# Router scratch in a PSUM bank, and 64-column products set between 512-column ones, in a fused attention and expert kernel

## The chip, the cores and the metric

The kernel runs on one core of a Trainium2 chip, in one launch. The metric is the device time of an execution in microseconds (us); less is better. Three runs of the kernel before took 832.63, 827.26 and 828.55 us, median 828.55.

The engines are named as in the profile: PE (TensorE, matrix products; PEld are its weight loads), DVE (VectorE), ACT (ScalarE), POOL (GpSimd) and SP (SyncE, which issues DMAs).

## The reference

Causal attention over 8 batches, 8 heads, 576 positions and 64 features, with a bias from a running sum of `s`; then a mixture of 8 experts, where each of the 4608 tokens goes to the one expert of the largest logit.

```python
def _attn_ref(q, k, v, s):
    scores = scale * np.matmul(q, k.transpose(0, 1, 3, 2))
    cum = np.cumsum(np.maximum(s, 0.0), axis=-1)
    bias = -(cum[:, :, :, None] - cum[:, :, None, :])
    scores = np.where(causal, -1000000000.0, scores + np.minimum(bias, 0.0))
    attn = np.exp(scores - np.max(scores, axis=-1, keepdims=True))
    attn = attn / (np.sum(attn, axis=-1, keepdims=True) + 1e-09)
    return np.matmul(attn, v)
def _moe_ref(x, expert_emb, tau, w1, w2):
    logits = xn @ en.T / tau                       # rows of x and of expert_emb normalised
    expert_idx = np.argmax(logits, axis=1)
    gate_w = softmax(logits)[np.arange(N), expert_idx]
    for e in range(E):
        mask = expert_idx == e
        h = np.maximum(x[mask] @ w1[e], 0.0)       # 512 -> 1024
        out[mask] = gate_w[mask, None] * (h @ w2[e])   # 1024 -> 512
```

## The kernel before

**Attention half.** The 64 heads are steps `n`, eight to a batch. A step computes scores for the row maxima of a later head (tiles `s`, read by DVE at lines 369, 406 and 409), the scores and exponentials of head `n` (tiles `ta`, `tb` in the pool `ps_t`), and the products with V of head `n - 2` (`pv`, lines 525 to 527), which add up in one fixed PSUM bank, `om`, columns 0 to 364. POOL subtracts the rounded exponentials from the full ones (line 251) for a second, low part of the products. Two or three steps behind, DVE normalises `om` into the token rows `xt` (lines 538 to 550).

When a batch of eight heads is done, `router(b, xt)` puts small steps into a queue of tasks, from which each step takes up to four at its end: `sume` adds up the logits (line 79 in the trace) into `L`, 128x40; `sel1` to `sel4` pick the best expert; `sel5` (line 622) compares and writes the one-hot rows `oh`; a few products on PE count ranks into `om` (columns 368 to 415), and DVE adds them up (lines 638 to 650); then POOL scatters the token rows to their experts' places in memory. `L`, `T` and `w` are parts of an SBUF tile named `idx`, which POOL fills and from which eight DMAs read a block of zeros early on, in `setup4`.

**Expert half.** An expert has places for 640 tokens, in tiles of 128. Its first layer is eight blocks `m` of 128 hidden features (`l1`, line 891): 12 products of 512 columns (tokens 0 to 511), since each number is kept as a high and a low half and three of the four products count. Tokens 512 to 575 are 12 products of 64 columns for each of the eight blocks, 96 in one burst (`l1a` calls `lpart`, line 915), issued behind block 5 for expert 1 and behind block 2 from expert 2 on. Tokens from 576 on are taken only where an expert has so many (`l1b`, a branch on PE). `lrect` applies the ReLU to the 64-column sums. The second layer (`l2`, line 967) has 24 products of 512 columns for each 128 tokens; its last tile is `l2t`, whose result is finished in the next expert's first layer (`l2u`). Expert 0 starts while the last batch is still being routed: its tokens are taken in three parts, `l1` with `lo` at 0, 256 and 384.

The order of the work on every engine is the order in which the program is written. Beside the first layer of expert `e`, DVE and ACT convert the second layer's weights to halves (lines 867 and 875); `xload` has POOL gather the token rows of expert `e + 1` (line 737; the first three behind block 2), and `xprep` splits and transposes them by DMAs that SP issues (line 788).

[...] The first layer's `h` uses half of a `ps_t` tile.

Of the kernel before, what the change touches and what calls it, by code (L numbers as in the profile page):

```python
# [8 lines left out]
F32 = mybir.dt.float32  # L9
# [8 lines left out]
PSUM = bass.MemoryType.PSUM  # L18
# [96 lines left out]
def main(ctx, tc, qkh, qkc, vtin, s_in, emb, tau, w1h, w2h, out, shared, nb):  # L115
# [5 lines left out]
    ps_s = ctx.enter_context(tc.tile_pool(name="ps_s", bufs=2, space=PSUM))  # L121
    ps_t = ctx.enter_context(tc.tile_pool(name="ps_t", bufs=2, space=PSUM))
    ps_m, om = shared["ps_m"], shared["om"]
# [474 lines left out]
    def router(b, xt):  # L598
        R = {}

        def sume():
            R["L"] = IX["L"].rearrange("p (j e) -> p j e", j=5)
            esum(nc, R["L"], xt[:, :, 0:XW])
# [5 lines left out]
        def sel2():  # L609
            T = R["T"] = IX["T"].rearrange("p (j e) -> p j e", j=5)  # L610
            nc.vector.tensor_tensor(T, R["L"], R["m"][:, 0].unsqueeze(2).to_broadcast([128, 5, NE]), op=ALU.is_ge)

# [3 lines left out]
        def sel4():  # L616
            R["w"] = IX["w"]
            nc.vector.tensor_reduce(R["w"], R["T"], AX.X, ALU.max)

# [174 lines left out]
    def pxm():  # L794
        return ps_m.tile([128, 512], F32, tag="m", name="pxm")

    def pxs():
        return ps_s.tile([128, 512], F32, tag="s", name="pxs")
# [84 lines left out]
    def l1(m, e, lo, hi, mid=None):  # L883
        wH, wL = ready(1, e, m)
        xH, xL = X[("H", e)], X[("L", e)]
        if isinstance(xL, tuple):
            xL = xL[lo > 0 or e > 0]
        h = (pxs() if e == 0 and m in {0: (1, 3, 5, 7), SPL: (1, 3, 5), SPM: (1, 2, 5)}[lo] else ps_t.tile([128, 2, 512], F32, tag="t", name="h")[:, 0])[:, 0:hi - lo]
        for c in range(4):
            for k, (w, x) in enumerate(((wH, xH), (wH, xL), (wL, xH))):  # L890
                nc.tensor.matmul(h, w[:, 128 * c:128 * c + 128], x[:, c, lo:hi], start=(c == 0 and k == 0), stop=(c == 3 and k == 2))  # L891
            if c == 1 and mid:
                mid()
        hH, hL = (t[:, lo:hi] for t in htile(m))
        nc.scalar.activation(hH, h, AF.Relu)
        nc.vector.scalar_tensor_tensor(hL, h, 0.0, hH, op0=ALU.max, op1=ALU.subtract)
# [10 lines left out]

    def lpart(e, u, h):
        xH, xL = X[("H", e)], X[("L", e)][1]
        lo = MAIN + HALF * u  # L910
        for m in range(8):
            wH, wL = ready(1, e, m)
# [10 lines left out]

    def l1a(e):
        h = pxs()
        lpart(e, 0, h)
        lrect(0, h)

    def l1b(e, h):
# [6 lines left out]
    def l1t():  # L936
        h = ps_t.tile([128, 2, 512], F32, tag="t", name="h")
        with tc.If(X["n", 0] == 1) as arm:
            for u in range(2):
                lpart(0, u, h[:, u])  # L940
        with arm.Else():
            for u in range(2):
                nc.tensor.matmul(h[:, u], wt(1, 0)[0][:, 0:128], X[("H", 0)][:, 0, 0:MAIN], start=True, stop=True)
        X["h", 0] = h
# [33 lines left out]
    def l2(e, t, mid={}):  # L978
        y = pxs()
        l2m(t, y, mid)  # L980
        l2o(e, t, y)
# [489 lines left out]
    for u in range(2):  # L1471
        lrect(u, X["h", 0][:, u])
    for e in range(NE):
        nx = e + 1 < NE
        w2, w1 = 16 * e + 8, 16 * e + 16
        for m in range(8):
# [3 lines left out]
            if e == 1 and m == 0:  # L1480
                l2o(0, NTL - 1, X["y", 0])
            if e and m == (5 if e == 1 else 2):
                l1a(e)
                size(e)
# [44 lines left out]
            if e == 3 and m == 4:  # L1529
                shared["total"] = nc.values_load(shared["ci"][0:1, NE - 1:NE], min_val=0, max_val=NT // 128)  # L1530
        if e:
            l1b(e, pxs())
        for t in range(0 if e else NF, NTL):
# [165 lines left out]
```

## Time and profile before

| | |
|---|---|
| runs | 832.63, 827.26, 828.55 us, median 828.55 |
| the profiled execution | 827.8 us, of which the span from first to last instruction is 826.1 us |
| PE busy | 769.1 us, 93% of the span |
| DVE, ACT, POOL busy | 556.5, 569.2 and 395.3 us |
[...]
| memory traffic | 140 GB/s over the span |

Times in the trace count from the start of the span. The attention half lasts to about 380 us, the expert half to the end. A row of the timeline gives the start, the length, the engine, the line of the kernel, the operation, what it writes and reads, how many equal ones stand behind each other, and in brackets the idle time of the engine ahead of it with what ended that. A product's length in the timeline is its latency; products overlap, so the distance of two starts is what one costs. Where the idle time is put down to "issue", the engine waited for nothing that the profile shows.

### The profile page before, as it was taken

The page shows a single profiled execution, that of the slowest core. Times are in us where ns is not written, and L with a number is a line of the kernel's source. Part 1 is how long each engine was busy: PE and PEld are TensorE (multiplying, and loading weights), DVE is VectorE, ACT ScalarE, POOL GpSimd, SP SyncE. Part 2 cuts the span into 40 slices and gives each one's busy share as a digit, 9 for nine tenths or more (in the row PEclk, how much of TensorE's full clock was granted, in tenths as well). Part 3 has the DMA queues.
Part 4 walks back from the last instruction along what each step waited for, and adds up shares of the span by engine and source line. Part 5 has one row for each costly group of instructions (what it writes and reads, how often), then busy time and mean ns, then how long its engine had stood idle before and what let it go on. Part 6 is the DMA issues. An engine that isn't in the chain of part 4 may idle for free. (4 is left out here: it accounts for less than half of the span.)

```text
span 826.1 us, 20954 instructions
## 1 busy us (share of the span) xinstructions
PE 769.1 (93%) x7998; PEld 552.9 (67%) x7998; DVE 556.5 (67%) x1818; ACT 569.2 (69%) x1029; POOL 395.3 (48%) x375
## 2 busy tenths in 40 slices
PE   8998898989989898999789998989989989999997
PEld 4798897989989897988454554545444544554554
DVE  7787788787878888898557765654555556645621
ACT  9898688897969897887467865827637649376410
POOL 9997596887869796873432121220221112202001
PEclk9999899999989999999989999999999989999999
DMA  7798779595949797764534855643744746534001
GB/s 162 158 196 169 137 177 193 133 209 132 199 113 216 150 209 150 177 207 129 185 99 154 190 160 158 163 153 108 177 145 112 188 151 140 177 113 124 25 13 53
DMA packets 76002, 124.01 MB, mean 150 GB/s; under 512 B 38823, under 2 KB 39231, under 8 KB 75032
## 3 DMA queue, kind: packets, MB, share of 16 engines
q0 software_dynamic: 19632, 69.69, 36.2%
q1 hardware_dynamic: 56260, 52.84, 24.1%
q8 instruction: 71, 1.16, 0.6%
q14 instruction: 39, 0.32, 0.1%
HBM read 93.99 MB, written 21.49 MB: 140 GB/s over the span
## 5 line engine op out<-in xcount | busy, mean ns | idle before, releaser
L251 POOL TENSOR_TENSOR PL<-P 128x576 f16<-128x576 f32 (+2 forms) x128 | 205.1, 1709 | 31.9 <-ACT P L500 21.7
L891 PE MATMUL h<-xH,wt 128*128 128x512 f16 (+2 forms) x560 | 155.7, 360 | 0.8 <-DVE hq L922 0.3
L891 PEld LDWEIGHTS <-wt 128*128 128x128 f16 x960 | 86.8, 100 | 84.6 <-issue 11.9
L975 POOL DMA_INDIRECT out<-Kx,xj x39 | 44.1, 1130 | 195.2 <-DVE Kx L974 165.4
L361 PE MATMUL s<-qkb 96*128 96x288 f32 (+4 forms) x272 | 98.7, 377 | 22.4 <-DVE M L369 21.8
L525 PE MATMUL om<-vh,P 128*128 128x73 f16 x960 | 110.5, 201 | 3.0 <-DVE xt L550 2.3
L737 POOL DMA_INDIRECT Qx<-xs,idx x40 | 44.3, 1107 | 140.1 <-ACT vjunk L830 70.7
L526 PE MATMUL om<-vl,P 128*128 128x72 f16 x960 | 109.7, 199 | 0.0
L527 PE MATMUL om<-vh,PL 128*128 128x73 f16 x960 | 109.5, 200 | 0.0
L526 PEld LDWEIGHTS <-P 128*128 128x128 bf16 x960 | 96.5, 101 | 4.2 <-issue 3.6
L525 PEld LDWEIGHTS <-P 128*128 128x128 bf16 x960 | 95.7, 101 | 0.5 <-DVE xt L550 0.3
L527 PEld LDWEIGHTS <-PL 128*128 128x128 f16 x960 | 95.7, 100 | 0.0
L891 PE MATMUL h<-xL,wt 128*128 128x512 f16 (+1 forms) x264 | 94.9, 366 | 0.0
L967 PE MATMUL pxs<-wt,hq 128*128 128x512 f16 x360 | 90.3, 384 | 3.3 <-DVE wt L875 3.3
L500 ACT ACTIVATE P<-tb 128x1024 f32<-128x1024 f32 x64 | 65.1, 1018 | 24.8 <-PE tb L466 23.4
L369 DVE CUSTOM_DVE_ANT_0 junk<-s,mS 128x448 bf16<-128x448 f32 (+3 forms) x144 | 73.9, 520 | 5.3 <-PE s L361 3.2
L967 PE MATMUL pxs<-wt,hp 128*128 128x512 f16 x288 | 74.5, 387 | 0.0
L361 PEld LDWEIGHTS s<-qkb 96*128 96x128 f32 x272 | 51.9, 194 | 29.8 <-DVE M L369 27.9
L974 DVE TENSOR_SCALAR Kx<-pxs,xj,idx 128x512 f32<-128x512 f32 x39 | 31.5, 808 | 54.8 <-PE pxs L967 31.7
L967 PEld LDWEIGHTS <-hq 128*128 128x128 f16 x360 | 35.5, 99 | 46.5 <-ACT vjunk L749 3.6
L463 PE MATMUL tb<-QC,KC 128*128 128x448 f32 (+3 forms) x256 | 64.5, 310 | 0.0
L459 PE MATMUL tb<-qkb 128*128 128x448 f32 (+3 forms) x256 | 62.0, 289 | 0.0
(309 smaller groups left out, 1962.1 us busy)
## 6 DMA issues: line engine op xcount, KB each, us to landing
qkb<-qkh POOLq DMA_DIRECT2D x15, 1216.0 KB
ring<-w2h SPq DMA_DIRECT2D x44, 256.0 KB
ring<-w1h SPq DMA_DIRECT2D x36, 256.0 KB
KC<-qkh POOLq DMA_DIRECT2D x14, 576.0 KB
QC<-qkh POOLq DMA_DIRECT2D x14, 576.0 KB
vT<-vtin SPq DMA_DIRECT2D x24, 320.0 KB
rw<-w1h SPq DMA_DIRECT2D x15, 256.0 KB
rw<-w2h SPq DMA_DIRECT2D x12, 256.0 KB
```

Source lines behind the costliest of these rows:

```text
L251: nc.gpsimd.tensor_tensor(out, a, b_, op=ALU.subtract)
L361: nc.tensor.matmul(out, G[g]["QB"][0:96, h, 128 * i:128 * i + 128], G[g]["KB"][0:96, h, lo:hi], start=True, stop=True)
L369: nc.vector.tensor_tensor_reduce(out=jk, in0=src, in1=ms, scale=1.0, scalar=NEG, op0=ALU.add, op1=ALU.max, accum_out=MP[n // 2][:, n % 2, ...
L459: nc.tensor.matmul(out, G[g]["KB"][:, h, ks:ks + 128], G[g]["QB"][:, h, 64 + qlo:64 + qhi], start=start, stop=False)
L463: nc.tensor.matmul(out, HD[n]["KC"][:, ks:ks + 128], HD[n]["QC"][:, qlo:qhi], start=False, stop=stop)
L500: nc.scalar.activation(HD[n]["P32"][:, 576:1600], HD[n]["tb"], AF.Exp, scale=0.125)
L525: nc.tensor.matmul(out, lh, vh[:, kb], start=(kb == 0), stop=False)
L526: nc.tensor.matmul(out[:, u:u + 72], lh, vl[:, kb], start=False, stop=False)
L527: nc.tensor.matmul(out, ll, vh[:, kb], start=False, stop=(kb == j))
L737: ins = nc.gpsimd.indirect_dma_start(out=x.bitcast(I32), out_offset=None, in_=src, in_offset=bass.IndirectOffsetOnAxis(ap=X[("i", e, t)][1 ...
L891: nc.tensor.matmul(h, w[:, 128 * c:128 * c + 128], x[:, c, lo:hi], start=(c == 0 and k == 0), stop=(c == 3 and k == 2))
L967: nc.tensor.matmul(y, h, w, start=(m == 0 and k == 0), stop=(m == 7 and k == 2))
```

## The change

Four things change. For batches 0 to 5 the router's `L`, `T` and `w` lie in the bank `om` (columns 416 to 500); batches 6 and 7 keep the SBUF tile. From expert 1 on, a bank `X["a"]` from `pxs()` is held through the first layer, and each 64-column product is issued right behind the 512-column product with the same weights; expert 1 begins this at block 2, behind a burst for blocks 0 and 1, the others at block 0. The ReLU of these sums moves behind the last block, and `l1a` is gone. After the first part of expert 0 the pool `ps_t` is closed, and its four banks become four tiles of one bank, from `pe()`; the first layer's `h` uses them, and the first output tile of the second layer from expert 1 on.

```diff
--- before.py
+++ after.py
@@ -119,7 +119,8 @@
     const = ctx.enter_context(tc.tile_pool(name="const", bufs=1))
     p2 = ctx.enter_context(tc.tile_pool(name="p2", bufs=2))
     ps_s = ctx.enter_context(tc.tile_pool(name="ps_s", bufs=2, space=PSUM))
-    ps_t = ctx.enter_context(tc.tile_pool(name="ps_t", bufs=2, space=PSUM))
+    ps_ts = ExitStack()
+    ps_t = ps_ts.enter_context(tc.tile_pool(name="ps_t", bufs=2, space=PSUM))
     ps_m, om = shared["ps_m"], shared["om"]
 
     P32s = [const.tile([128, 1664], F32, name=f"P32{i}") for i in range(3)]
@@ -599,7 +600,7 @@
         R = {}
 
         def sume():
-            R["L"] = IX["L"].rearrange("p (j e) -> p j e", j=5)
+            R["L"] = (IX["L"] if b > nb - 3 else om[:, 416:456]).rearrange("p (j e) -> p j e", j=5)
             esum(nc, R["L"], xt[:, :, 0:XW])
 
         def sel1():
@@ -607,14 +608,14 @@
             nc.vector.tensor_reduce(m[:, 0], R["L"], AX.X, ALU.max)
 
         def sel2():
-            T = R["T"] = IX["T"].rearrange("p (j e) -> p j e", j=5)
+            T = R["T"] = (IX["T"] if b > nb - 3 else om[:, 456:496]).rearrange("p (j e) -> p j e", j=5)
             nc.vector.tensor_tensor(T, R["L"], R["m"][:, 0].unsqueeze(2).to_broadcast([128, 5, NE]), op=ALU.is_ge)
 
         def sel3():
             nc.vector.tensor_tensor(R["T"], R["T"], wval, op=ALU.mult)
 
         def sel4():
-            R["w"] = IX["w"]
+            R["w"] = IX["w"] if b > nb - 3 else om[:, 496:501]
             nc.vector.tensor_reduce(R["w"], R["T"], AX.X, ALU.max)
 
         def sel5():
@@ -794,6 +795,12 @@
     def pxm():
         return ps_m.tile([128, 512], F32, tag="m", name="pxm")
 
+    def pe():
+        if "pe" not in X:
+            ps_ts.close()
+            X["pe"] = ctx.enter_context(tc.tile_pool(name="ps_e", bufs=4, space=PSUM))
+        return X["pe"].tile([128, 512], F32, tag="e", name="pe")
+
     def pxs():
         return ps_s.tile([128, 512], F32, tag="s", name="pxs")
 
@@ -885,10 +892,16 @@
         xH, xL = X[("H", e)], X[("L", e)]
         if isinstance(xL, tuple):
             xL = xL[lo > 0 or e > 0]
-        h = (pxs() if e == 0 and m in {0: (1, 3, 5, 7), SPL: (1, 3, 5), SPM: (1, 2, 5)}[lo] else ps_t.tile([128, 2, 512], F32, tag="t", name="h")[:, 0])[:, 0:hi - lo]
+        a0 = 2 if e == 1 else 0 if e else 8
+        if m == a0:
+            X["a"] = pxs()
+            lpart(e, 0, X["a"], range(a0))
+        h = (pe() if e or lo else pxs() if m % 2 else ps_t.tile([128, 2, 512], F32, tag="t", name="h")[:, 0])[:, 0:hi - lo]
         for c in range(4):
             for k, (w, x) in enumerate(((wH, xH), (wH, xL), (wL, xH))):
                 nc.tensor.matmul(h, w[:, 128 * c:128 * c + 128], x[:, c, lo:hi], start=(c == 0 and k == 0), stop=(c == 3 and k == 2))
+                if m >= a0:
+                    nc.tensor.matmul(X["a"][:, HALF * m:HALF * m + HALF], w[:, 128 * c:128 * c + 128], x[:, c, hi:hi + HALF], start=(c == 0 and k == 0), stop=(c == 3 and k == 2))
             if c == 1 and mid:
                 mid()
         hH, hL = (t[:, lo:hi] for t in htile(m))
@@ -905,10 +918,10 @@
         X["n", e] = nc.values_load(shared["cn"][0:1, e:e + 1], engines=[mybir.EngineType.PE], min_val=0, max_val=1,
                                    skip_runtime_bounds_check_because="the result of a comparison is 0 or 1")
 
-    def lpart(e, u, h):
+    def lpart(e, u, h, ms=range(8)):
         xH, xL = X[("H", e)], X[("L", e)][1]
         lo = MAIN + HALF * u
-        for m in range(8):
+        for m in ms:
             wH, wL = ready(1, e, m)
             for c in range(4):
                 for k, (w, x) in enumerate(((wH, xH), (wH, xL), (wL, xH))):
@@ -921,11 +934,6 @@
         nc.scalar.activation(hH, h, AF.Relu)
         nc.vector.scalar_tensor_tensor(hL, h, 0.0, hH, op0=ALU.max, op1=ALU.subtract)
 
-    def l1a(e):
-        h = pxs()
-        lpart(e, 0, h)
-        lrect(0, h)
-
     def l1b(e, h):
         with tc.If(X["n", e] == 1) as arm:
             lpart(e, 1, h)
@@ -934,13 +942,13 @@
         lrect(1, h)
 
     def l1t():
-        h = ps_t.tile([128, 2, 512], F32, tag="t", name="h")
+        h = [pe() for u in range(2)]
         with tc.If(X["n", 0] == 1) as arm:
             for u in range(2):
-                lpart(0, u, h[:, u])
+                lpart(0, u, h[u])
         with arm.Else():
             for u in range(2):
-                nc.tensor.matmul(h[:, u], wt(1, 0)[0][:, 0:128], X[("H", 0)][:, 0, 0:MAIN], start=True, stop=True)
+                nc.tensor.matmul(h[u], wt(1, 0)[0][:, 0:128], X[("H", 0)][:, 0, 0:MAIN], start=True, stop=True)
         X["h", 0] = h
 
     def l2z():
@@ -976,7 +984,7 @@
                                      in_=ys, in_offset=None, bounds_check=NT - 1, oob_is_err=False)
 
     def l2(e, t, mid={}):
-        y = pxs()
+        y = pe() if e and t == 0 else pxs()
         l2m(t, y, mid)
         l2o(e, t, y)
 
@@ -1469,7 +1477,7 @@
     l2(0, 1, {2: third, 4: partial(l2o, 0, 0, y), 6: fifth})
     l2(0, 2, {2: fourth, 7: l1t})
     for u in range(2):
-        lrect(u, X["h", 0][:, u])
+        lrect(u, X["h", 0][u])
     for e in range(NE):
         nx = e + 1 < NE
         w2, w1 = 16 * e + 8, 16 * e + 16
@@ -1479,8 +1487,7 @@
                 l2u(e - 1)
             if e == 1 and m == 0:
                 l2o(0, NTL - 1, X["y", 0])
-            if e and m == (5 if e == 1 else 2):
-                l1a(e)
+            if e and m == 2:
                 size(e)
             if e == 1:
                 wsq(w2 + (6, 7, 8)[m] if m < 3 else w1 + (0, 0, 0, 1, 4)[m - 3])
@@ -1529,6 +1536,7 @@
             if e == 3 and m == 4:
                 shared["total"] = nc.values_load(shared["ci"][0:1, NE - 1:NE], min_val=0, max_val=NT // 128)
         if e:
+            lrect(0, X["a"])
             l1b(e, pxs())
         for t in range(0 if e else NF, NTL):
             if nx:
```

On DVE, at the end of the step in which batch 1's comparison falls (`vl` is the low part of V, `idx` the SBUF tile, `z` the first normalising step of the next head), before:

```order
L310 SCALAR_TENSOR_TENSOR vl<-V,sc,vh_108 128x3x144 [waits Activation_49]
L618 TENSOR_REDUCE idx<-idx 128x5
L622 TENSOR_TENSOR oh<-wsel,idx 128x40 [waits DVE_49]
L538 TENSOR_SCALAR z<-om 128x5 [waits PE_49]
L369 ISA junk,M<-s_2467,mS 128x448 [waits PE_49]
```

and now:

```order
L311 SCALAR_TENSOR_TENSOR vl<-V,sc,vh_108 128x3x144 [waits Activation_49]
L619 TENSOR_REDUCE om<-om 128x5 [waits PE_49]
L623 TENSOR_TENSOR oh<-wsel,om 128x40 [waits DVE_49]
L539 TENSOR_SCALAR z<-om 128x5
L370 ISA junk,M<-s_2467,mS 128x448 [waits PE_49]
```

The places are the same. The wait for PE has moved from line 538 to the reduction two instructions ahead of it. PE's own instructions, and the places of its waits, are the same in the whole attention half.

On PE, in the first layer of expert 2 (`h` and `pe` are the 512-column sums, `pxs` the 64-column ones, `xH` and `xL` the halves of the tokens), the end of block 2 and the start of the burst before:

```order
L891 MATMUL h_8872<-xH_8329,wt_6219 128x512
L891 LDWEIGHTS wt_6219
L891 MATMUL h_8872<-xL_8330,wt_6219 128x512
L891 LDWEIGHTS wt_6219
L891 MATMUL h_8872<-xH_8329,wt_6219 128x512
L915 LDWEIGHTS wt_6219
L915 MATMUL pxs_8887<-xH_8329,wt_6219 128x64
L915 LDWEIGHTS wt_6219
L915 MATMUL pxs_8887<-xL_8330,wt_6219 128x64
```

and the start of a block now:

```order
L902 LDWEIGHTS wt_6219
L902 MATMUL pe_8851<-xH_8308,wt_6219 128x512
L904 LDWEIGHTS wt_6219
L904 MATMUL pxs_8814<-xH_8308,wt_6219 128x64
L902 LDWEIGHTS wt_6219
L902 MATMUL pe_8851<-xL_8309,wt_6219 128x512
L904 LDWEIGHTS wt_6219
L904 MATMUL pxs_8814<-xL_8309,wt_6219 128x64
```

The 64-column products stand one by one between the long ones, each still with a weight load of its own. PE has 16,059 rows in the one order and in the other.

## Rows read from the trace of the kernel before

**Rows 1.** The page: busy us, share of the span and instructions of each engine.

```profile
PE 769.1 (93%) x7998; PEld 552.9 (67%) x7998; DVE 556.5 (67%) x1818; ACT 569.2 (69%) x1029; POOL 395.3 (48%) x375
```

**Rows 2.** Busy time by stretch: two batches of eight heads, and 32 undisturbed us.

```profile
core 0: us, PE busy (x) PEld busy (x) DVE busy (x) ACT busy (x) POOL busy (x), PEclk, DMA share, GB/s
171.38:216.15 44.77, 41.40 (x590) 40.31 (x586) 36.99 (x141) 37.18 (x49) 35.05 (x30) 0.96 0.77 170
262.53:304.72 42.19, 39.99 (x589) 38.93 (x586) 35.74 (x141) 37.05 (x49) 35.24 (x30) 1.00 0.85 177
282.00:314.00 32.00, 31.98 (x471) 31.32 (x470) 26.51 (x110) 29.32 (x37) 27.22 (x25) 1.00 0.87 190
```

**Rows 3.** Waits of PE, 60 to 380 us: total us, times, longest.

```profile
PE s L361 <- DVE M L369: 21.5, 9, 3.4
```

**Rows 4.** Timeline of PE, batch 1: the product behind a long wait.

```profile
141.75 0.40 PE L361 MATMUL s<-qkb 96*128 96x288 f32 x1 [3.33 <-DVE M L369]
```

**Rows 5.** Timeline of DVE, 135 to 143.5 us, batch 1.

```profile
136.20 0.66 DVE L310 SCALAR_TENSOR_TENSOR vl<-V,sc,vh 128x432 f16<-128x432 f32 x1
136.78 0.18 DVE L618 TENSOR_REDUCE idx<-idx 128x5 f32<-128x40 f32 x1
137.00 4.08 DVE L622 TENSOR_TENSOR oh<-wsel,idx 128x40 bf16<-128x40 f32 x1
141.01 0.15 DVE L538 TENSOR_SCALAR z<-om 128x5 f32<-128x5 f32 x1
```

**Rows 6.** Timeline of POOL, 129 to 143 us.

```profile
135.52 3.36 POOL L251 TENSOR_TENSOR PL<-P 128x576 f16<-128x576 f32 x2
138.46 1.38 POOL L338 DMA_DIRECT2D QC<-qkh  x1
139.12 1.90 POOL L251 TENSOR_TENSOR PL<-P 128x576 f16<-128x576 f32 x1
```

**Rows 7.** Groups of DVE, 90 to 340 us: busy us, mean ns, idle before.

```profile
L622 DVE TENSOR_TENSOR oh<-wsel,idx 128x40 bf16<-128x40 f32 x6 | 23.3, 3887 | 0.2
...
L638 DVE TENSOR_TENSOR idx<-om,base 128x40 f32<-128x40 f32 x6 | 1.2, 200 | 2.6 <-PE om L527 2.6
```

**Rows 8.** Stretches, columns as in rows 2: PE's lower clock after two waits.

```profile
94.90:101.70 6.80, 6.47 (x72) 6.35 (x72) 3.42 (x15) 3.29 (x5) 1.89 (x1) 0.50 0.48 85
142.70:146.00 3.30, 3.30 (x40) 3.23 (x37) 1.48 (x10) 2.88 (x4) 1.90 (x1) 0.50 0.50 92
```

**Rows 9.** Stretches: 60 first-layer products of expert 7, and six such sets.

```profile
778.41:791.36 12.95, 12.95 (x66) 5.87 (x63) 7.15 (x16) 5.55 (x10) 0.00 (x0) 1.00 0.01 1
sum 84.96, PE 84.96 PEld 37.01 DVE 46.96 ACT 59.03 POOL 3.12; mean PE 14.16 PEld 6.17 DVE 7.83 ACT 9.84 POOL 0.52
```

**Rows 10.** Stretches: the 64-column bursts of experts 1 and 3, and all seven.

```profile
455.02:457.82 2.80, 2.80 (x97) 2.79 (x96) 2.15 (x4) 0.80 (x3) 0.00 (x0) 1.00 0.79 225
...
552.90:559.23 6.33, 3.83 (x97) 3.22 (x96) 2.87 (x12) 0.60 (x1) 3.92 (x4) 0.99 0.73 218
...
sum 38.75, PE 26.26 PEld 23.10 DVE 18.65 ACT 4.39 POOL 20.04; mean PE 3.75 PEld 3.30 DVE 2.66 ACT 0.63 POOL 2.86
```

**Rows 11.** Timeline of PE, expert 3: the burst, a gap, the product behind.

```profile
552.90 0.19 PE L915 MATMUL pxs<-xH,wt 128*128 128x64 f16 x1
...
555.38 0.19 PE L915 MATMUL pxs<-xH,wt 128*128 128x64 f16 x1 [0.51 <-issue]
...
559.23 0.61 PE L891 MATMUL h<-xH,wt 128*128 128x512 f16 x1
```

**Rows 12.** Timeline of POOL, 552 to 559 us: first and last of three gathers.

```profile
554.05 1.04 POOL L737 DMA_INDIRECT Qx<-xs,idx  x1 [0.30 <-ACT hq L895]
...
556.73 1.00 POOL L737 DMA_INDIRECT Qx<-xs,idx  x1 [0.31 <-issue]
```

**Rows 13.** Timeline of PE's weight loads in a clean burst, expert 3, line 915.

```profile
573.80 2.84 PEld L915 LDWEIGHTS <-wt 128*128 128x128 f16 x95
```

**Rows 14.** Timeline of SP, 515 to 560 us: expert 3's last transposing DMA.

```profile
531.07 1.23 SPq L788 DMA_TRANSPOSE xL<-xr  x1
```

**Rows 15.** Timeline of DVE, 540 us: the fourth output tile of expert 2.

```profile
539.71 0.81 DVE L974 TENSOR_SCALAR Kx<-pxs,xj,idx 128x512 f32<-128x512 f32 x1 [3.05 <-PE om L857]
```

## The prediction

> **What bounds the kernel now.** I read the busy times first, then the stretches of both halves, then the waits of TensorE (PE), and last the instructions around its longest waits. PE is busy for 769.1 of the 826.1 us span [rows 1], and in an undisturbed stretch of the attention half for 31.98 of 32 us, while ScalarE has 29.32, VectorE 26.51 and GpSimd 27.22 [rows 2]. PE is the bound, so a gap of PE or a time at its lower clock is lost, and work that leaves another engine gains only where PE waited for it.
>
> Attention half: nearly all that PE waits for between 60 and 380 us is one thing, VectorE's release of a score tile: 21.5 us in nine waits [rows 3]. One such wait is 3.33 us long, before the product at 141.75 [rows 4]. VectorE was late there because of one small instruction: the one-hot comparison of the router at line 622, 128x40 elements, took 4.08 us (137.00 to 141.08), where its neighbour on as many elements took 0.18 [rows 5]. GpSimd ran two subtractions and issued a DMA in that time, and the last subtraction ended at 139.12 + 1.90 = 141.02, with which the comparison ended too [rows 6]. The comparison reads both inputs from SBUF. The instruction at line 310, which reads one input from PSUM, ran 136.20 to 136.86 inside a GpSimd subtraction and took 0.66 us [rows 5, 6]. Over the middle batches the comparison costs 3.887 us on average, while the addition at line 638, with one input in PSUM, costs 0.200 [rows 7]. [...]
>
> Expert half: PE has no gap in a normal first layer, and 60 products of 512 columns take 12.95 us [rows 9]. The 96 products of 64 columns at line 915 take 2.80 us in a clean burst and 6.33 in a disturbed one [rows 10]. In the disturbed one PE sits idle 0.4 to 0.5 us before every few products, with nothing to wait for that the profile shows [rows 11]. These gaps begin when GpSimd issues three gathers in a row, 554.05 to 557.73 [rows 12]. The bursts of experts 1 and 7 have no such gathers beside them and no gaps, and the transfers alone are not the cause: the clean burst of expert 1 runs beside a DMA share of 0.79, the disturbed one beside 0.73 [rows 10]. From 559.23 the products of 512 columns come at half rate (0.61 us long) for 3.4 us: the gaps have cost the clock too [rows 11].
>
> **The change part by part.**
>
> *Router scratch in PSUM.* For batches 0 to 5 the comparison and its neighbours get one input from PSUM. I price each at 0.2 us, as at line 638 [rows 7]. The comparison then gives back 3.7 us of VectorE time per batch, more than any wait of PE behind it, so the whole wait goes. Of the 21.5 us, two short waits (0.8 us together) come from other work and stay; the first batch's wait of 1.9 us at 81.88 goes too, since the reduction behind it no longer writes a block of SBUF which GpSimd and eight DMAs held. That is 20.7 us. The stretches at the lower clock that follow add 2 x 6.8 + 3 x 3.3 = 23.5 us [rows 8], in which PE did half of what it could: 11.7 us. Sum: 32.4 us. A check: the batch of 44.77 us held one wait of 3.3 and one stretch of 3.3, so 39.8 would remain; the one of 42.19, at full clock throughout, held a wait of 2.2, so 40.0 [rows 2]. They agree.
>
> The price of it: three VectorE instructions per batch now wait for PE's last product in the bank, 18 in all. Line 638 already waits so: 2.6 us in five times [rows 7], 0.43 us a wait by the average of all six. That bounds the new waits between nothing and 7.8 us. I take nothing: the reduction at 136.78 starts when PE's products into this bank have just ended, and the line behind it (538) waited for the same products before [rows 5]. What is queued behind a longer wait is VectorE's reduction of the next scores, for which PE waits, so its upper end counts in full.
>
> [...]
>
> *64-column products behind their 512-column ones.* Experts 2 to 7 lose their burst at the third block; expert 1 keeps 24 of its 96 products as a short burst. Both orders issue the same products and weight loads. In a clean burst a product of 64 columns with its load costs 2.80 / 96 = 0.029 us [rows 10], and 95 loads lie in 2.84 us, 0.030 each [rows 13], so a load can hide even behind the short product. I price an interleaved product at 0.029 as well. Seven bursts took 38.75 us against 7 x 2.80: 19.15 us go [rows 10]. The 60 products behind six of them took 84.96 us against 6 x 12.95: 7.26 us go with the lower clock [rows 9]. Sum: 26.4 us, from experts 2 to 6. No row shows a short product between two long ones; the bounds are 0.029 and the 0.066 of the disturbed burst [rows 10], which would lose 672 x 0.037 = 25 us again. I take the lower: at 552.90 the change from long to short products costs no extra time [rows 11]. Below it nothing is to be had, since 64 columns need their time.
>
> The interleaved products need the fifth token tile's columns some 8 us earlier, at the start of the layer instead of its third block. For the layer of the burst at 552.90, which began about 545, the last transposing DMA was issued at 531.07 [rows 14]; that covers it. The 64-column sums now hold a bank through the layer. It is that of the fourth output tile, which VectorE had read out at 540.52, 4.5 us before [rows 15]. Their ReLU moves to the layer's end; it is needed by the last tile of the second layer, four tiles of 24 products later. Costed at nothing.
>
> *Four one-bank tiles.* They serve the first layer, which has no gaps now: nothing. Their first use waits for the last two-bank tile's reader, beside a product block; nothing, or a fraction of a us.
>
> **Sum:** 827.8 (the profiled execution) - 32.4 - 26.4 = 769.0 us. The median of the three runs is 828.55, 0.75 above that execution, so 769 to 770; I say **769**.
>
> **The rivals.**
>
> 1. *The gathers starve the interleaved stream too.* In the disturbed burst some 24 products with 24 loads came through in the 4 us of gaps: 12 instructions per us. The interleaved stream wants 4 in 0.245 us, 16.3 per us, so it is 17 short over 4 us, 1.1 us, unless enough are queued. With a fall of the clock (7.26 / 5 = 1.5 us) in each of five experts that is 13 us: 782. For it: PE's gaps have no releaser. Against: products of 512 columns beside gathers show no gap, and 96 short ones ran before the supply thinned.
> 2. *The comparison is slow for another reason*, or the new waits take its place: only the expert half gains, 801. For: it outlasted two GpSimd instructions and a DMA issue. Against: its end coincides with GpSimd's, and line 310 passes freely [rows 5, 6].
> 3. *Another resource takes half of the attention gain*: ScalarE has 29.32 of 32 us and DMA a share of 0.87 in the undisturbed stretch [rows 2], and today's waits let both catch up. Half of 32.4 kept: 785. Against: that stretch runs 32 us at PE's pace.
> 4. *The weight loads show.* Over the program loads average 552.9 / 7998 = 0.069 us [rows 1]. If that holds behind a product of 64 columns, 0.040 us appear 672 times, 27 us: 796. [...]
> [...]
>
> **How the numbers follow.** Forecast 0.73, rivals 1 to 5: 0.10, 0.06, 0.05, 0.03, 0.03. The forecast's own range is 763 to 780: below it by the short waits and other catching up, above it by the new waits and a part of the gaps. Rivals 1 and 3 extend it to 788: 762 to 788 holds 0.85 or so. This kernel's runs cannot tell less than about 1% from no change, so faster means under 820: the forecast and rivals 1 to 3, and most of 4, make 0.95; same 0.02; slower 0.03.
>
> **What would show it.** Right: the comparison at 0.2 us, no wait of PE for a score tile above 0.5 us in batches 0 to 5, batches near 39.8 us; first layers of experts 2 to 7 at about 23.5 us without gaps and at full clock. Wrong: gaps of 0.4 us beside the three gathers, a new wait of VectorE at the scratch reductions, products of 512 columns 0.07 us further apart behind short ones, or a lower clock inside the layer.

## The result, and the profile after

The changed kernel takes 767.42 us (median, 766.65 to 769.66), the kernel before beside it 827.9: a ratio of 0.928, 95% interval 0.922 to 0.934. Forecast were 769 us in a range of 762 to 788. The profiled execution took 766.73 us with a span of 764.9; that of before took 827.8, so by the spans 61.2 us are gone.

The page's busy times and its row of PE's granted clock, to be held against [rows 1]:

```profile
PE 742.7 (97%) x7998; PEld 538.7 (70%) x7998; DVE 530.8 (69%) x1818; ACT 567.5 (74%) x1029; POOL 392.7 (51%) x375
...
PEclk9999999999999999999999999999999999999999
```

PE is still the bound and now works for 97% of the span; its mean granted clock is 0.993, where it was 0.966. VectorE lost 25.7 us of work, the slow comparisons and a little more; ScalarE and GpSimd did the same work within 3 us.

**Attention half.** Two batches by stretch (columns as in rows 2), taken from one comparison to the next, and the waits of PE between 60 and 360 us (total us, times, longest):

```profile
128.26:167.97 39.71, 39.68 (x587) 38.93 (x586) 32.72 (x141) 36.92 (x49) 34.97 (x31) 1.00 0.87 193
247.36:287.88 40.52, 40.00 (x587) 39.02 (x586) 32.83 (x141) 36.91 (x49) 35.59 (x31) 1.00 0.91 190
```

```profile
PE om L526 <- DVE xt L551: 2.0, 1, 2.0
PE s L362 <- DVE M L370: 0.6, 2, 0.4
```

Batches that took 44.77 and 42.19 us [rows 2] take 39.71 and 40.52 (the first window here is one batch earlier than that of rows 2), with PE idle for 0.03 and 0.52 us and the clock at 1.00 in both. The waits for score tiles went from 21.5 us in nine to 0.6 in two [rows 3]. The 2.0 us in the first line belong to the end of the half; a later section comes back to them. Last, VectorE's groups between 85 and 310 us (busy us, mean ns, idle before):

```profile
L639 DVE TENSOR_TENSOR om<-om,base 128x40 f32<-128x40 f32 x6 | 1.2, 207 | 0.0
...
L623 DVE TENSOR_TENSOR oh<-wsel,om 128x40 bf16<-128x40 f32 x6 | 1.2, 196 | 0.2
...
L619 DVE TENSOR_REDUCE om<-om 128x5 f32<-128x40 f32 x6 | 1.2, 195 | 0.0
```

The comparison (line 623 now) fell from 3,887 ns to 196 [rows 7], and no instruction on the scratch is seen to wait for PE: the idle time ahead of each such group is 0.2 us or less over its five or six batches, as in the kernel before, and no releaser is named for it.

**Expert half.** The first layer of expert 3, with its 64-column products between the long ones, by stretch, and GpSimd's gathers in the midst of it:

```profile
504.77:528.55 23.78, 23.63 (x198) 12.16 (x197) 14.34 (x34) 14.69 (x33) 5.80 (x5) 1.00 0.48 146
```

```profile
514.45 1.04 POOL L738 DMA_INDIRECT Qx<-xs,idx  x1 [0.30 <-ACT hq L908]
515.79 1.02 POOL L738 DMA_INDIRECT Qx<-xs,idx  x1 [0.30 <-issue]
517.12 1.51 POOL L738 DMA_INDIRECT Qx<-xs,idx  x1 [0.31 <-issue]
```

192 products take 23.78 us, PE is idle for 0.15 of them, and the clock stays at 1.00 through the three gathers that had broken up the burst of before [rows 10 to 12].

### The profile page after: what moved, and what is told of

It is laid out like the page before. It is cut to its first block, busy times and chain, and to the rows that moved or that the text cites. A ratio compares the mean times of both kernels' runs of the same rounds, so it can differ in the third digit from the quotient of the medians.

```text
span 764.9 us, 20947 instructions
## 1 busy us (share of the span) xinstructions
PE 742.7 (97%) x7998; PEld 538.7 (70%) x7998; DVE 530.8 (69%) x1818; ACT 567.5 (74%) x1029; POOL 392.7 (51%) x375
## 5 line engine op out<-in xcount | busy, mean ns | idle before, releaser
L902 PE MATMUL pe<-xH,wt 128*128 128x512 f16 (+1 forms) x576 | 153.2, 344 | 0.5 <-PEq L1010 0.5
L902 PEld LDWEIGHTS <-wt 128*128 128x128 f16 x960 | 85.9, 98 | 81.7 <-issue 2.2
L526 PE MATMUL om<-vh,P 128*128 128x73 f16 x960 | 107.6, 199 | 2.6 <-DVE xt L551 2.0
L527 PE MATMUL om<-vl,P 128*128 128x72 f16 x960 | 107.1, 197 | 0.5 <-issue 0.4
L527 PEld LDWEIGHTS <-P 128*128 128x128 bf16 x960 | 95.0, 99 | 3.6 <-issue 3.2
L902 PE MATMUL pe<-xL,wt 128*128 128x512 f16 (+1 forms) x288 | 96.0, 344 | 0.0
L526 PEld LDWEIGHTS <-P 128*128 128x128 bf16 x960 | 94.1, 99 | 0.2
L904 PE MATMUL pxs<-xH,wt 128*128 128x64 f16 x432 | 83.3, 193 | 0.0
L975 PE MATMUL pxs<-wt,hq 128*128 128x512 f16 x297 | 72.9, 379 | 3.3 <-DVE wt L882 3.3
L904 PEld LDWEIGHTS <-wt 128*128 128x128 f16 x648 | 63.5, 98 | 0.4
L908 ACT ACTIVATE hp<-pe 128x512 f16<-128x512 f32 (+1 forms) x27 | 14.2, 525 | 64.3 <-PE pe L902 55.5
L874 ACT ACTIVATE wt<-ring,idx 128x512 f16<-128x512 f32 x80 | 53.7, 711 | 10.1 <-DVE idx L864 7.7
```

Of the source, the lines that this page charges most:

```text
L526: nc.tensor.matmul(out, lh, vh[:, kb], start=(kb == 0), stop=False)
L527: nc.tensor.matmul(out[:, u:u + 72], lh, vl[:, kb], start=False, stop=False)
L874: nc.scalar.activation(h, a, AF.Copy, scale=s)
L904: nc.tensor.matmul(X["a"][:, HALF * m:HALF * m + HALF], w[:, 128 * c:128 * c + 128], x[:, c, hi:hi + HALF], start=(c == 0 and k == 0), sto ...
L975: nc.tensor.matmul(y, h, w, start=(m == 0 and k == 0), stop=(m == 7 and k == 2))
```

## The experiments

Two families of runs came out, and they split by chip. On chip 2 the kernel before takes 827.5 us (median of 11), as in the times shown; on chips 10, 3 and 6 it takes 800.8, 802.2 and 801.7. The chip of the first runs is not recorded. The order was 10, 2, 3, 6, and each chip was met in one sitting only, so a chip cannot be told from its sitting. Each ratio below is against the kernel before on the same chip.

**The scratch alone** (chip 10): the kernel before with the three pieces of scratch moved.

```diff
-            R["L"] = IX["L"].rearrange(...)
+            R["L"] = (IX["L"] if b > nb - 3 else om[:, 416:456]).rearrange(...)
...
-            R["w"] = IX["w"]
+            R["w"] = IX["w"] if b > nb - 3 else om[:, 496:501]
```

> The first part alone: the kernel before, with the router scratch of batches 0 to 5 in the PSUM bank. Theory (the comparison was held by GpSimd because both its inputs lay in SBUF, and PE stood behind it): the comparison falls from 3.9 to 0.2 us, the nine waits for score tiles and the stretches at the lower clock behind them go, the attention half gives its 32 us: 795 to 797 us; first layers as before, with 6.3 us bursts. Rival (the parts need each other, or ScalarE and the DMA queues eat a share that the shortened expert half later hides): 805 to 812. Rival (the gain came with the pool of one-bank tiles): about 828.

It took 767.97 us beside 800.77, ratio 0.959 (0.956 to 0.962): 32.8 us. That is the forecast's 32.4 for this part, but it lands at 768, where only the whole change should have landed. All eleven bursts of 64-column products are clean here, 2.96 us each, although the expert half is word for word that of before. The burst of expert 3 by stretch (line 915 alone: us, PE, PEld, clock, DMA), and GpSimd beside it:

```profile
515.25:518.21 2.96, 2.96 (x96) 2.84 (x95) 1.00 0.57 201
```

```profile
516.39 1.04 POOL L737 DMA_INDIRECT Qx<-xs,idx  x1 [0.30 <-ACT hq L895]
517.74 1.02 POOL L737 DMA_INDIRECT Qx<-xs,idx  x1 [0.30 <-DVE idx L102]
519.07 0.99 POOL L737 DMA_INDIRECT Qx<-xs,idx  x1 [0.31 <-issue]
```

The first gather is issued 1.14 us into the burst and the third 3.82, as in [rows 11, 12] (1.15 and 3.83). The same instructions in the same places, 96 products in 2.96 us from first start to last end, no gap.

**The other parts alone** (chip 10): the changed kernel with all scratch back in SBUF.

```diff
-            R["L"] = (IX["L"] if b > nb - 3 else om[:, 416:456]).rearrange(...)
+            R["L"] = IX["L"].rearrange(...)
```

and the same for the two others.

> The other parts alone: the changed kernel with the router scratch back in SBUF (interleaved 64-column products and four one-bank tiles kept). Theory: the comparison takes 3.9 us again and PE waits some 21 us for score tiles; only the expert half gains, 25 us in experts 1 to 7 and perhaps the 4.6 us of expert 0: 797 to 802 us. Rival (expert 0's 4.6 us came from the attention half's better timing): 802. Rival (the two gains overlap): below 795.

801.0 us beside 800.77, ratio 1.000 (0.998 to 1.002). Nothing gained, nothing lost: on a chip without gaps the interleaving and the tiles are worth nothing, and an interleaved short product costs what it costs in a burst. The forecast of 797 to 802 us came out for another reason than its own: it counted on 25 us of gain from 827, and here the kernel before takes 801. In the trace the comparison takes 3,832 ns again and PE waits 21.5 us in nine for score tiles.

**The four one-bank tiles alone** (chip 10): the burst `l1a` kept, the tiles of the first layer from the new pool.

```diff
-        h = (pxs() if e == 0 and m in {...}[lo] else ps_t.tile(...)[:, 0])[:, 0:hi - lo]
+        h = (pe() if e or lo else pxs() if m % 2 else ps_t.tile(...)[:, 0])[:, 0:hi - lo]
```

> The four one-bank tiles alone: the kernel before with the tiles of the first layer, from expert 0's second part on, drawn from four one-bank tiles; the 64-column products stay in their burst. Theory (PE had no gaps there, tiles were never late): no change, 826 to 829 us, bursts 6.3 us beside the gathers as before. Rival (expert 0's 4.6 us come from tiles that are free earlier): 823 to 824, with expert 0 at 44 us instead of 48.7. Rival (a part of the 25 us of the expert half is the tiles): 815 or less.

800.47 us beside 800.77, ratio 1.000 (0.999 to 1.002): no change, as forecast, on this chip; beside gaps it did not run.

**The changed kernel on chip 2.**

> The changed kernel itself, on a chip on which the kernel before is run too. On the chip of the first four experiments the kernel before took 801 us instead of 828 and its bursts of 64-column products had no gaps (2.96 us from first to last, beside three gathers); there the scratch alone gave 768 and the other parts alone gave nothing. Theory (the gaps beside the gathers are the chip's, and the interleaving only hides them): where the kernel before takes about 801, the changed one takes 766 to 769, ratio 0.957 to 0.960; where it takes 828, 767 again, ratio 0.928. Rival (the expert half's gain adds to the scratch wherever it runs): 742 to 745 beside 801.

767.1 us beside 827.5, ratio 0.928 (0.924 to 0.932): the first result again.

**The weights w alone in the PSUM bank** (chip 2): only the last line of the first diff.

> The kernel before with one of the three pieces of scratch alone in the PSUM bank: the weights w of batches 0 to 5, so that the comparison reads one input from PSUM; sums and thresholds stay in SBUF. Theory (only the two SBUF inputs of the comparison cost): as the whole scratch, the comparison 0.2 us, 0.960 of the kernel before (769 beside 801), at most 2 us more for the first batch's short wait. Rival (the reductions and the multiplication around it are held as well): a part of the gain only, 780 to 795 beside 801.

798.24 us beside 827.5, ratio 0.964 (0.958 to 0.971): 29.3 us. The group of the comparison, one of its neighbours, and PE's waits between 60 and 360 us:

```profile
L611 DVE TENSOR_TENSOR idx<-idx,rm 128x40 f32<-128x40 f32 x6 | 3.6, 604 | 0.0
...
L622 DVE TENSOR_TENSOR oh<-wsel,om 128x40 bf16<-128x40 f32 x6 | 1.2, 195 | 0.2
```

```profile
PE s L361 <- DVE M L369: 3.7, 4, 1.9
```

One input in PSUM is enough for the comparison: 195 ns. The subtraction at line 611, which keeps two inputs in SBUF, costs 604 ns against 202 in the changed kernel, so it too ran longer, by 0.4 us; the wait of 1.9 us in the first batch stays. Nothing in the expert half is changed, and chip 2 shows the gaps: the burst of expert 3 by stretch, GpSimd beside it, and PE's gaps:

```profile
524.16:531.21 7.05, 4.63 (x96) 3.77 (x95) 0.88 0.73 224
```

```profile
525.31 1.05 POOL L737 DMA_INDIRECT Qx<-xs,idx  x1 [0.30 <-ACT hq L895]
526.66 1.02 POOL L737 DMA_INDIRECT Qx<-xs,idx  x1 [0.30 <-issue]
527.99 1.00 POOL L737 DMA_INDIRECT Qx<-xs,idx  x1 [0.31 <-issue]
```

```profile
526.62 0.19 PE L915 MATMUL pxs<-xL,wt 128*128 128x64 f16 x1 [0.49 <-issue]
...
527.38 0.19 PE L915 MATMUL pxs<-xL,wt 128*128 128x64 f16 x1 [0.51 <-issue]
...
528.14 0.20 PE L915 MATMUL pxs<-xH,wt 128*128 128x64 f16 x1 [0.45 <-issue]
...
528.89 0.23 PE L915 MATMUL pxs<-xH,wt 128*128 128x64 f16 x2 [0.43 <-issue]
...
529.65 0.23 PE L915 MATMUL pxs<-xL,wt 128*128 128x64 f16 x1 [0.44 <-issue]
```

Against the same burst on chip 10: the first gather again 1.15 us in, issues of the same length, but PE gets a few products every 0.76 us. The five bursts with three gathers beside them take 6.8 to 7.5 us, the six others 2.96.

**w alone back in SBUF** (chip 2): the changed kernel, one line.

```diff
-            R["w"] = IX["w"] if b > nb - 3 else om[:, 496:501]
+            R["w"] = IX["w"]
```

> The changed kernel with w alone back in SBUF, the sums and thresholds still in the PSUM bank. Is the comparison then an instruction with two SBUF inputs again? It reads a table in SBUF and w. Theory: it takes 3.9 us again and the attention half's gain goes: 797 to 802 us, as the kernel before where that takes 801. Rival (any scratch in the bank moves the order enough): 766 to 775.

797.51 us beside 827.5, ratio 0.965 (0.959 to 0.971). VectorE's group, and PE's waits between 60 and 360 us:

```profile
L623 DVE TENSOR_TENSOR oh<-wsel,idx 128x40 bf16<-128x40 f32 x5 | 19.3, 3855 | 0.2
```

```profile
PE s L362 <- DVE M L370: 19.3, 7, 3.4
```

One operand of 128x5 elements moved back, and 3.9 us a batch and 19.3 us of waits return: 30.4 us more than the changed kernel on this chip. The rest of the change is worth 30.0 us here (827.5 - 797.51) and nothing on chip 10.

Two SBUF inputs alone do not make the comparison slow. Batches 6 and 7 keep them in SBUF in the changed kernel too: in its first trace batch 7's comparison takes 0.19 us at 355.38, with GpSimd idle since 351.30, and batch 6's takes 0.49 at 325.33, ending where GpSimd passes from one subtraction to the next (325.72). So its length goes with GpSimd's subtractions, and how many of them it sits out differs. That rests on the traces: no run moved those subtractions.

**Delayed gathers** (chips 10, 3 and 6): GpSimd kept busy until the burst is over.

```diff
             if nx and e > 0 and m == 2:
+                for _ in range(8 if e > 1 else 0):
+                    nc.gpsimd.memset(mS, 0.0)
                 for t in range(3):
                     xload(e + 1, t)
```

> The kernel before with eight GpSimd memsets of about 0.64 us each ahead of the three gathers of experts 3 to 8, so that the gathers are issued some 5 us later, after the burst of 64-column products; nothing else is moved. Theory (PE starves in the burst because the three gathers are issued beside it): the bursts take 2.80 us again, the clock does not fall behind them, and the five disturbed layers give back up to 25 us: 802 to 806 us; where the delay misses a burst, that one stays at 6.3. Rival (the burst runs dry by its own short products, whatever GpSimd does): bursts stay at 6.3 us, 828. Rival (the gathers starve whatever PE runs, long products too): gaps of 0.4 us appear among the 512-column products, about 820.

> The delayed gathers once more: the kernel before with eight GpSimd memsets ahead of the three gathers of experts 3 to 8. The first time it met a chip on which no burst has gaps (kernel before 801 us). Where the kernel before takes 828 and its bursts 6.4 to 7.5 us beside the gathers: theory (the gathers beside the burst make the gaps) five bursts of 2.96 us, no lower clock behind them, 801 to 806 us; rival (the 64-column products run dry on such a chip whatever GpSimd does) bursts stay, 828; rival (the gathers starve 512-column products as well) gaps 5 us later, 815 to 828. Where the kernel before takes 801: 801 again.

> The delayed gathers, for a chip on which the kernel before takes 828 us. Theory (the three gathers beside the burst make the gaps): five bursts of 2.96 us from first to last instead of 6.4 to 7.5, 801 to 806 us. Rival (the 64-column products run dry there whatever GpSimd does): bursts stay, 828. Rival (delayed gathers starve the 512-column products): gaps 5 us later, 815 to 828. Beside 801: 801 again, and the question stays open.

Beside 800.77, 802.17 and 801.74 it took 800.71, 801.8 and 801.55, ratios 1.000, 0.999 and 1.000 (all within 0.997 to 1.003). The gathers came 3.2 us after the burst's end (first at 550.86, the burst from 544.70 to 547.66), but all three chips were of the kind without gaps, so there was nothing to win. (The gathers delayed are those for experts 3 to 7, counted from 0, where the texts say 3 to 8.) That the gathers make the gaps rests on the traces of the other kind alone, as does what delaying them would do there.

**The weight arithmetic moved**, two attempts. At 335.30 us, VectorE takes 3.87 us for a subtraction of two SBUF inputs that takes 0.74 at its next place (340.53); VectorE, GpSimd and PE in the changed kernel's first trace:

```profile
335.30 3.87 DVE L882 SCALAR_TENSOR_TENSOR wt<-rw,idx,wt 128x512 f16<-128x512 f32 x1
```

```profile
335.60 3.02 POOL L252 TENSOR_TENSOR PL<-P 128x576 f16<-128x576 f32 x2
```

```profile
340.67 0.20 PE L526 MATMUL om<-vh,P 128*128 128x73 f16 x1 [1.98 <-DVE xt L551]
```

It is the comparison's case once more: GpSimd's two subtractions end at 338.62, VectorE's at 339.17, and PE stands 1.98 us. The first attempt (chip 2) moved the step of one loop turn:

```diff
-        if n < NH:
+        if n < NH - 1:
             wlow(1)
...
             for f in (norm1, norm2, norm3):
                 f(n - 2)
+            if n == NH - 1:
+                wlow(1)
```

> The changed kernel with one step moved: the last piece of weight arithmetic in the attention half, which subtracts two SBUF inputs on VectorE and took 3.87 us beside one GpSimd subtraction (normally 0.74), comes behind the norms. Theory (the same contention as in the comparison): the 3.87 us fall to 0.74, PE's wait of 2.0 us at the score tile and the fall of its clock for 3.4 us behind it go, 3.7 us faster than the changed kernel: 764 beside 767.5. Rival (the piece meets another GpSimd subtraction at its new place, or PE's wait passes to the next step): no change, 766 to 769.

767.48 us beside 827.5, where the changed kernel took 767.1: no change. It was the wrong turn; the instruction at 335.37 still took 3.87 us, and what moved was its successor of 0.74. (PE's wait of 2.0 us is ahead of the products into `om`, not at a score tile as the text has it.) The second attempt (chip 3) took the turn before:

```diff
-        if n < NH:
-            wlow(1)
+        if n < NH and n != NH - 2:
+            wlow(1 if n < NH - 2 else 2)
```

> The changed kernel with the weight arithmetic that took 3.87 us beside a GpSimd subtraction moved behind the next normalisation of VectorE, 3 us later, when that subtraction has ended (the earlier attempt had moved its successor, and the 3.87 us stayed). Theory: 0.74 to 1.5 us there, PE's wait of 2.0 us before the products into the output bank and the clock's fall behind it go: 764 to 765.5 us. Rival (PE is held by the next thing at that place, or the clock's fall comes from elsewhere): 766.5 to 768.

765.57 us (765.3 to 766.74) beside 802.17, ratio 0.955 (0.953 to 0.958). VectorE's two instructions at the new place, one directly behind the other, and PE's largest waits from 300 to 360 us:

```profile
337.62 2.54 DVE L882 SCALAR_TENSOR_TENSOR wt<-rw,idx,wt 128x512 f16<-128x512 f32 x2
```

```profile
PE V L300 <- DVE vl L311: 0.5, 1, 0.5
PE pxs L766 <- DMA Qx<-xs,idx: 0.4, 1, 0.4
```

The wait of 2.0 us is gone, as the theory has it. But GpSimd's subtractions had not ended at the new place, as the text expected: they run to 338.95, and the first of the two instructions still takes 1.88 us (337.62 to 339.50). Whether the kernel is faster than the changed one this run does not show: the changed kernel did not run on chip 3.

**The changed kernel on chip 6.**

> The changed kernel once more, for a chip on which the kernel before takes 801 us (its bursts without gaps); so far the changed kernel itself ran beside 828 only. Theory (there the expert half has nothing to give): 766 to 769 beside 801, ratio 0.957 to 0.960, as the scratch alone gave; the kernel with the moved weight arithmetic, 765.6 on such a chip, is 1.5 to 2 us below it. Rival (the interleaving is worth its 25 us anywhere): 742 to 745. Beside 828: 767 again.

766.95 us beside 801.74, ratio 0.957 (0.955 to 0.960). So the changed kernel takes the same on both kinds of chip. The moved arithmetic (765.57) stands 1.4 us below it by medians, with ranges that overlap (765.75 to 768.57 here). By the traces it reaches expert 0's first long products at 343.09 instead of 344.26, and spends 60.21 instead of 59.43 us from there to expert 1, so a part of its gain was lost again, to what was not followed up.

## Why the prediction was right, and where not

**The scratch** was priced at 32.4 us: 20.7 of waits, 11.7 of clock. The second of these counts five stretches at a clock of 0.50 between 60 and 380 us in the trace of before: two of 6.8 us, from 94.9 and 231.4, and three of 3.3, from 142.7, 187.1 and 320.2. Up to expert 0's second part the change gained 31.5 (390.74 to 359.22 us in the two traces); alone it gave 32.8 on chip 10, and w alone undone on chip 2 cost 30.4. The mechanism holds by its strongest test, the one small operand that switches nearly the whole loss on and off (29.3 us gained with w alone in the bank, 30.4 lost with w alone back in SBUF). The check by batches (39.8 and 40.0) met 39.71 and 40.52, the second with 0.52 us of idle PE. What it missed is the weight arithmetic at 335.30: it is a second row of the same kind, and it stood in the trace of before, 3.87 us at 367.70 with PE's wait of 1.98 us ahead of 373.06. That wait, with a stretch of 3.4 us at a clock of 0.50 behind it (from 341.3), is what is left of this loss.

**The new waits on the bank** were priced at nothing, with 7.8 us as the bound. The idle time ahead of each group of scratch lines is 0.2 us or less in six batches. The wait for PE stands in the changed kernel's order, ahead of the reduction at line 619, and the time measured ahead of that line (0.0 us) decides for nothing.

**The interleaving** was priced at 26.4 us: 19.15 in the bursts, 7.26 of clock behind them. From expert 1's start to the end the two traces differ by 25.1 us, and the first layers take 23.78 us for 23.5 forecast: 0.28 us over 96 pairs, so a pair takes 0.248 for 0.245, and the short product costs about 0.03 as in a burst, not 0.066. But this term is a property of the kind of chip that the shown times came from. On chip 10 the bursts are clean beside the same gathers, and the term is 0; on chips 3 and 6 no trace has a burst beside three gathers, but the kernel before takes 802 us there as well. The prediction never asked whether the gaps belong to the program; one trace could not tell it. That the changed kernel was then measured beside a kernel before of 827.9 us was luck in this respect: on chip 6 the forecast gain of 58.8 us would have been 24 too much (34.8 measured).

**Not in the sum:** 4.6 us in expert 0, from its second part to expert 1 (48.72 to 44.09 us). The waits for gathered tokens there were shorter and a stretch at the lower clock was missing. No experiment isolates it. Between executions with the same code this stretch varies: in the three traces of the delayed gathers, which have the code of before there, it took 46.64, 50.01 and 46.90 us (chips 10, 3 and 6). So most of it may be scatter; on chip 2 it took 46.79 us with w alone in the bank and 44.44 in the changed kernel, and the cause stays open. It made up for what the attention half (0.9) and the experts (1.3) fell short, and put the profiled execution 2.3 us below the 769.0 of the sum; that the misses nearly cancel is luck.

**The tiles and the moved ReLU** at nothing: the tiles alone gave ratio 1.000, and all the parts outside the scratch together gave 1.000, on a chip without gaps.

**The rivals.** The gathers do not starve the interleaved stream (rival 1): PE is idle 0.15 us in 23.78 on the first chip, and the same on chip 2. The estimate of 16.3 wanted and 12 supplied per us did not come out; whether instructions were queued ahead or the supply was better is not shown. The comparison was not slow for another reason (rival 2): see both runs with w alone, and what stands behind the second. ScalarE and DMA did not eat half of the gain (rival 3): PE was busy for 39.68 of 39.71 us and for 40.00 of 40.52, at a DMA share of 0.87 and 0.91. Weight loads did not show (rival 4): a pair of a long and a short product with its two loads takes 0.248 us (23.78 / 96), where the rival's 0.040 us on top of 0.245 would have made 0.285. A lower clock inside the layer, the last 0.03 of the chances, did not come: it is 1.00 in the layer shown and 0.99 on average from expert 1's start to the end.

## What to carry to other kernels

A small VectorE instruction that takes 4 us where its neighbours take 0.2 (3,887 ns beside 200 here) is worth more attention than any large one: look at where both its inputs lie, what GpSimd runs then, and whether both end together; moving one input to PSUM, 128x5 elements, brought the instruction to 195 ns and PE's waits for score tiles from 21.5 us to 3.7 here, and after the fix one should look for the next row of the same kind. A gap that no semaphore explains may belong to the chip, not the program (the same program took 827.5 us on chip 2 and 800.8 on chip 10): profile the kernel on a second chip before a change that only mends such gaps is counted as a gain, and quote the gain with the chip. An order that never issues short products alone (long and short in turn) cost nothing on chip 10 (ratio 1.000), and with it the kernel takes the same 767 us on chip 2, which has the gaps, and on chip 6.

## What the runs showed of the hardware

**Two kinds of chip.** The kernel before takes 827.5 us on chip 2 and 801 to 802 on chips 10, 3 and 6, in 11 to 25 runs on each, all but one of them within 0.8% of their median; the changed one takes 767.1 and 766.95. The difference sits where GpSimd issues several indirect DMAs in a row. Not only PE stands still there: the changed kernel's five scatters near the start of expert 0, on chip 2, first GpSimd's first and last, then ScalarE:

```profile
362.86 1.01 POOL L670 DMA_INDIRECT xs<-xt,pos  x1 [11.14 <-DVE hp L909]
...
368.02 0.92 POOL L670 DMA_INDIRECT xs<-xt,pos  x1 [0.30 <-issue]
```

```profile
364.24 0.28 ACT L908 ACTIVATE hq<-pe 128x128 f16<-128x128 f32 x1 [0.85 <-PE pe L902]
366.50 0.28 ACT L908 ACTIVATE hv<-pe 128x128 f16<-128x128 f32 x1 [1.98 <-PE pe L902]
370.10 0.28 ACT L908 ACTIVATE hv<-pe 128x128 f16<-128x128 f32 x1 [3.32 <-remote]
```

And ScalarE at the same instructions on chip 6, where the scatters run from 360.57 to 366.89:

```profile
361.48 0.28 ACT L908 ACTIVATE hq<-pe 128x128 f16<-128x128 f32 x1 [0.39 <-PE pe L902]
362.15 0.28 ACT L908 ACTIVATE hv<-pe 128x128 f16<-128x128 f32 x1 [0.39 <-PE pe L902]
362.82 0.28 ACT L908 ACTIVATE hv<-pe 128x128 f16<-128x128 f32 x1 [0.39 <-PE pe L902]
```

On chip 2 these follow their predecessors (the first one that at 363.11) by 1.13, 2.26 and 3.60 us, on chip 6 by 0.67 each. The wait put down to PE ahead of 366.50 was for something else: PE's last product at line 902 ended at 365.09, 1.4 us before. PE itself had no gap there, but it then waits 3.3 us on chip 2 that it does not wait on chip 6, where it waits 8.5 us for gathered tokens instead of 3.4; the two sums, 6.7 and 8.5 us, are not far apart. What makes a chip of the one kind or the other, and whether it stays so, no run here shows. Nor is a way shown by which GpSimd's issues would hold PE and ScalarE: instruction fetches stand alike near the bursts of both kinds, one of 16 KB at 552.8 us beside the broken burst at 552.90 (before) and one at 515.2 beside the clean one at 515.25 (the scratch alone, chip 10). One more difference goes with the kind in every trace: the view of DMAs gives the gathers' time from issue to landing on chips 10, 3 and 6 (3.9 to 4.5 us in the median) and gives none for chip 2 and for the first two traces. What that means is open, but a reader of a single trace can see it.

**Who holds whom.** VectorE's subtraction at 335.30 had started 0.30 us before GpSimd's pair and still ended 0.55 us after it, at 3.87 us for 0.74; GpSimd's pair took 1.17 and 1.91 us, as its next pair at 341.33 did (1.18 and 1.92), beside which VectorE ran no such subtraction. A DMA issue of GpSimd alone did not hold VectorE: at 340.53 it took 0.74 us beside one (340.35 to 341.33). So the instruction that starts first in the trace was the one held here. A VectorE instruction with two inputs in SBUF was slow beside GpSimd's subtractions in the runs with w alone too: 3.855 us, against 0.195 with one input in PSUM. On chip 2 other engines stood still beside GpSimd's DMA issues: PE for 0.43 to 0.51 us at a time in the burst at 524.16, ScalarE for 1.98 us ahead of 366.50. Through what, no run shows.
